# A tuned H3 and MLP kernel: the statistics between two units from accumulator sums and powers, gating in stages, weights split ahead of the chain, products paused

## The chip, the core and the metric

The kernel runs on one core of a Trainium2 chip. The metric is device time in microseconds (us) of one execution. The core has five engines with a queue each: TensorE (PE; PEld is its loading of weights), VectorE (DVE), ScalarE (ACT), GpSimd (POOL) and SyncE (SP), which here issues the DMAs. Each works through its queue in order, and waits at an instruction until what it reads is there and the buffer that it writes is free. So an instruction that waits holds up all that stands behind it on its engine.

## The reference

Two layers, each of a mixer (A) and an MLP (B), on 2048 tokens of 1024 features in float32, with the same weights in both layers.

```
def _A_ref(q, k, v, shift_k, ssm_k, ssm_D):
    ...
    kv = k_shift * v
    ...
    y = y + kv * ssm_D[None, None, :]
    return q * y
def _B_ref(x, w1, b1, w2, b2):
    h = jnp.einsum("bsd,df->bsf", x, w1) + b1
    zero = jnp.zeros_like(h)
    r = jnp.where(h > zero, h, zero)
    h = r * r
    out = jnp.einsum("bsf,fd->bsd", h, w2) + b2
    return out
...
x = A_q
x = x + _A_ref(_layernorm(x, axis=-1), A_k, A_v, A_shift_k, A_ssm_k, A_ssm_D)
x = x + _B_ref(_layernorm(x, axis=-1), B_w1, B_b1, B_w2, B_b2)
x = x + _A_ref(_layernorm(x, axis=-1), A_k, A_v, A_shift_k, A_ssm_k, A_ssm_D)
x = x + _B_ref(_layernorm(x, axis=-1), B_w1, B_b1, B_w2, B_b2)
```

What is left out makes `k_shift`, a causal convolution of k with 4 taps, and `y`, a causal convolution of kv with ssm_k over all 2048 tokens, by FFT. `y` depends on k, v, ssm_k and ssm_D alone, not on x, so both layers use the same one.

## The kernel before

**Units.** The tokens are cut into four blocks of 512, a block into four tiles of 128. A unit is the MLP of one layer on one block. The table `ORDER` (L36) gives their order: (layer 0, block 0), (layer 1, block 0), (layer 0, block 1) and so on; the last two blocks of layer 1 end together. Units 0 and 1 have the same block: unit 1 needs what unit 0 gives, through a mixer and two layernorms. Only between these two does the **chain** (L1727) run.

**Steps.** A unit is a list of steps. A step of kind m1 (first product) or m2 (second) has 12 matmuls of 128x512 in units 0 and 1: each float32 factor is split into a high and a low part, and three of the four products are added (`mm3`, L355 to L358). At the end of unit 0 its last 28 steps are half steps: for two tiles (tiles 0 and 1, the first half) and then for the other two, with 6 matmuls each. Then follow 24 half steps of unit 1's m1, with 12 matmuls of half the width: 12 on the first two tiles, which do not need the other two, and 12 on those. The first 8 steps of unit 0 in the main loop are half steps too.

**Weights.** `w_advance` loads a weight by DMA, casts it to its high part on ACT (L1112), and subtracts to get the low part (the split, L1120) on DVE or POOL, by a table `WLO` and the phase: DVE in full steps and in the first half's m2, POOL in the second half's m2 (phase "b"), and POOL for three of four in the ahead steps of m1 (phase "x"). Some weights were stored split and come back whole (`whl<-wd_m`). The split runs three steps ahead of the matmuls (five in phase "x"), as far as six buffers `whl` allow.

**The chain.** At the end of a half, the result is added to the accumulator `acc` in two parts (`evict1`). Then mean and variance of the two tiles give a scale, y gates the scaled tile, the product is added, a second layernorm follows, and the normalized tiles are transposed and split into `xh` and `xl` for unit 1. These are stages, which `lag.at(d, stage, ...)` puts d steps later into the program; `lag.tick()` writes out what is due at a step. `CHAIN` (L67) holds the delays of the eleven stages for the first and for the second half.

**Beside it** run two streams, a piece per step. The forward stream (L374 to L515) transforms k, v and ssm_k for later blocks: on DVE three multiply-adds L386 and a product L388 into `fx`, which PE transposes (L441) into a bank `pt`, and for ssm_k the sums L504 and L505. The product stream (L540) multiplies the spectra on POOL (L546), reduces on DVE (L550), and ends in matmuls L616. `PACE_SLACK` sets how many steps it shall be done ahead of time; from it comes `pace`, the work per step. In half steps the loop's end takes a tenth of it:

```
rate = pace.get(u, 100) * (PREP_PACE if busy else 1.0)
if len(tts) < NT:
    rate *= 0.1
owed += rate
todo = min(owed, BURST * rate)
while todo > 0:
    x = next(pds, 0)
```

A product that is not ready to go gives None there, and the forward stream moves one piece on.

Of the kernel before, what the change touches and what calls it, by code (L numbers as in the profile page):

```python
# [20 lines left out]
P = 128  # L21
# [28 lines left out]
PACE_SLACK = {1: 74, 3: 10}  # L50
PACE_TO = {1: 2}
PLAIN = 1
PAD_C, PAD_P, PAD_M = 104, 56, 32
# [13 lines left out]
CHAIN = ((2, 3, 3, 7, 8, 8, 9, 13, 13, 14, 14), (2, 3, 3, 7, 8, 8, 9, 12, 12, 13, 13))  # L67
NORM = "VAVA"
# [181 lines left out]
def tile_h3_mlp(ctx: ExitStack, tc: tile.TileContext, q, kT, vT, shk, ssmT, ssmD, w1, b1, w2, b2,  # L250
# [1476 lines left out]
    def chain(accs, b, xh, xl, ready):  # L1727
        def bn(st, h):
            for n, tt in enumerate(st["tts"]):
                V.bn_stats(st["st"][:, n, h], accs[tt][:, h * 512:(h + 1) * 512])  # L1730

        def agg(st):
            mv = st["mv"] = pre.tile([P, 2, 2], F32, name="mv3", bufs=2)
            for n in range(2):
                V.bn_aggr(mv[:, n], st["st"][:, n])
            st["ve"], st["sd"] = rstd_a(mv)

        def newst(st):
            st["st"] = pre.tile([P, 2, 2, 6], F32, name="st3", bufs=2)

        def scales(st):
            r = st["r"] = rstd_b(st["ve"], st["sd"])
            st["nm"] = pre.tile([P, 2], F32, name="nm", bufs=3)
            V.scalar_tensor_tensor(st["nm"], st["mv"][:, :, 0], -1.0, r, op0=OP.mult, op1=OP.mult)

        def scaled(st, n):
            out = []
            for h in range(2):
                z = ps1()
                A.activation(z, accs[st["tts"][n]][:, h * 512:(h + 1) * 512], AF.Identity,  # L1750
                             bias=st["nm"][:, n:n + 1], scale=st["r"][:, n:n + 1])
                out.append((h, z, accs[st["tts"][n]][:, h * 512:(h + 1) * 512], st["y"][n][:, h * 512:(h + 1) * 512]))
            return out

        def gate(ops):
            for h, z, x, y in ops:
                V.tensor_mul(z, z, y)
            for h, z, x, y in ops:
                V.tensor_add(x, x, z)

        def spread_of(st, n, ops):
            for h, z, x, y in ops:
                V.bn_stats(st["st"][:, n, h], x)

        def evict1(st, os, dh):
            d = slice(dh * 512, (dh + 1) * 512)
            for n, tt in enumerate(st["tts"]):
                V.tensor_add(accs[tt][:, d], os[tt], accs[tt][:, d])
                V.bn_stats(st["st"][:, n, dh], accs[tt][:, d])

        def stage(st, k):
            tts = st["tts"]
            if k == 0:
                agg(st)
            elif k == 1:
                scales(st)
                newst(st)
            elif k == 2:
                ops = scaled(st, 0)
                gate(ops)  # L1780
                more = scaled(st, 1)
                spread_of(st, 0, ops)
                gate(more)
                spread_of(st, 1, more)
            elif k == 3:
                agg(st)
            elif k == 4:
                scales(st)
            elif k in (5, 6):
                n = k - 5  # L1790
                x, m, r = accs[tts[n]], st["mv"][:, n, 0:1], st["r"][:, n:n + 1]
                st["o", n] = []
                st["z", n] = [row() for _ in range(2)]
                for kh in range(2):
                    xn = st["z", n][kh]["t"]
                    xs = x[:, kh * 512:(kh + 1) * 512]
                    if NORM[2 * n + kh] == "A":
                        A.activation(xn, xs, AF.Identity, bias=st["nm"][:, n:n + 1], scale=r)
                    else:
                        V.tensor_scalar(xn, xs, m, r, op0=OP.subtract, op1=OP.mult)  # L1800
                    st["o", n].append(xn)
# [10 lines left out]
            else:  # L1812
# [552 lines left out]
```

## Time and profile before

| what | us |
|---|---|
| median of 3 runs (lowest, highest) | 2678.97 (2678.12, 2685.03) |
| the profiled execution | 2684.3 |
| its span, first to last instruction | 2682.5 |

The profile is of that one execution. Times within it are counted from the start of the span. Two stretches bear on the change: the main part of unit 0 with the end of the block before it, and the half steps with the chain.

| stretch, us | PE busy | DVE busy | ACT busy | POOL busy | PE clock granted |
|---|---|---|---|---|---|
| 130 to 450 | 307.82 | 265.12 | 140.98 | 176.75 | 0.98 |
| 450 to 560 | 101.25 | 84.45 | 50.68 | 42.49 | 0.97 |

A row of the timeline gives the start, the time taken, engine, line, operation, the tiles written and read, and in brackets how long the engine stood idle before it and what ended that. Matmuls overlap, so the time from one start to the next is what one costs. In the list of waits an entry gives total, times and longest.

### The profile page before, as it was taken

Reading aid. Unit: us, or ns where it says so; the run is one execution under the profiler, and the core shown is the slowest. Engines: PE = TensorE matmul, PEld = TensorE weight load, DVE = VectorE, ACT = ScalarE, POOL = GpSimd, SP = SyncE. Lnnn points to the kernel's source line nnn. Section 1 sums busy time; section 2 is a strip of 40 time slices with the busy share of each in tenths; the row PEclk is TensorE's granted clock in tenths of the full one; section 3 lists DMA queues with packets and bytes.
Section 4 is the critical chain, followed back from the end, with each engine's and each line's share of the span. In section 5 each row is a group of like instructions: output and inputs, shape, how many; then the busy total and the mean of one; then the engine's idle time right before and its main releaser. Section 6 shows DMA issues by size and latency. Waiting matters only on the chain.

```text
span 2682.5 us, 36122 instructions
## 1 busy us (share of the span) xinstructions
PE 2623.8 (98%) x12388; PEld 2199.4 (82%) x12388; DVE 1985.1 (74%) x2881; ACT 1124.1 (42%) x1915; POOL 1034.1 (39%) x675
## 2 busy tenths in 40 slices
PE   7999899899999999999999999999999999999999
PEld 6888787787888888888888888888788778888887
DVE  7979788788887878779767775456778668777553
ACT  3444244343435323343233422345444585454342
POOL 2436665155551744417454275100100217536111
PEclk9999999999999999999999999999999999999999
DMA  7789988689989998888987888689889797878653
GB/s 247 255 306 310 296 291 283 240 282 357 348 296 315 313 331 307 275 292 308 337 307 261 297 292 314 201 273 312 299 298 307 263 340 255 263 249 316 232 193 121
DMA packets 380265, 763.16 MB, mean 284 GB/s; under 512 B 44064, under 2 KB 159408, under 8 KB 377008
## 3 DMA queue, kind: packets, MB, share of 16 engines
q1 hardware_dynamic: 380080, 760.85, 83.0%
q8 instruction: 98, 1.61, 0.2%
q14 instruction: 87, 0.71, 0.1%
HBM read 583.49 MB, written 177.21 MB: 284 GB/s over the span
## 4 chain that ended last, share of the span: by engine, by line
PE 79%; DMA 8%; DVE 5%; POOL 2%; issue 2%; ACT 2%; SPq 1%; DVEq 0%; POOLq 0%; ACTq 0%
PE p L357 23%; PE p L356 23%; PE p L358 23%; DMA whl<-wd_m 2%; PE pt L358 2%; PE pt L357 2%; PE pt L356 2%; PE p L1194 2%; DMA wr<-w 2%; DMA cg<-gd 1%; DVE whl L1120 1%; POOL cp L546 1%; DMA wd_m<-whl 0%; PE p L817 0%; DVE sm L550 0%
## 5 line engine op out<-in xcount | busy, mean ns | idle before, releaser
L546 POOL TENSOR_TENSOR cp<-cx,cg 128x384 f32<-128x384 f32 (+5 forms) x288 | 542.0, 1895 | 574.7 <-DVE sm L550 362.2
L356 PE MATMUL p<-xh,whl 128*128 128x512 f32 (+1 forms) x1504 | 578.4, 385 | 5.6 <-DMA whl<-wd_m 5.6
L358 PE MATMUL p<-xh,whl 128*128 128x512 f32 (+1 forms) x1504 | 574.1, 382 | 3.3 <-DVE whl L1120 2.8
L357 PE MATMUL p<-xl,whl 128*128 128x512 f32 (+1 forms) x1504 | 574.1, 382 | 0.1
L1112 ACT CAST whl<-wr 128x512 fp32r<-128x512 f32 x546 | 332.5, 619 | 468.4 <-PE p L358 278.6
L1120 DVE TENSOR_TENSOR whl<-wr,whl 128x512 fp32r<-128x512 f32 x486 | 421.0, 877 | 135.0 <-ACT whl L1112 130.2
L356 PE MATMUL p<-whl,rh 128*128 128x512 f32 x1204 | 475.4, 395 | 6.0 <-DMA whl<-wd_m 5.2
L357 PE MATMUL p<-whl,rh 128*128 128x512 f32 x1204 | 471.2, 391 | 2.8 <-POOL whl L1120 1.7
L358 PE MATMUL p<-whl,rl 128*128 128x512 f32 x1204 | 470.6, 391 | 0.0
L356 PEld LDWEIGHTS p<-xh,whl 128*128 128x128 f32 x1504 | 284.7, 189 | 60.8 <-issue 4.9
L358 PEld LDWEIGHTS p<-xh,whl 128*128 128x128 f32 x1504 | 284.2, 189 | 58.2 <-DVE whl L1120 3.0
L357 PEld LDWEIGHTS p<-xl,whl 128*128 128x128 f32 x1504 | 284.5, 189 | 52.4 <-DVE xl L1507 0.3
L1597 DVE TENSOR_TENSOR rl<-wr,rh 128x512 fp32r<-128x512 f32 x140 | 138.6, 990 | 182.5 <-ACT rh L1594 182.4
L1120 POOL TENSOR_TENSOR whl<-wr,whl 128x512 fp32r<-128x512 f32 x60 | 86.7, 1448 | 484.4 <-ACT whl L1112 438.1
L356 PEld LDWEIGHTS p<-whl,rh 128*128 128x128 f32 x1204 | 227.3, 189 | 54.1 <-issue 3.3
L357 PEld LDWEIGHTS p<-whl,rh 128*128 128x128 f32 x1204 | 227.1, 189 | 50.2 <-DVE whl L1120 2.7
L358 PEld LDWEIGHTS p<-whl,rl 128*128 128x128 f32 x1204 | 227.0, 189 | 47.5
L550 DVE TENSOR_REDUCE sm<-cp 128x128 f32<-128x384 f32 (+5 forms) x288 | 249.4, 874 | 12.3 <-POOL cp L546 12.3
L1589 ACT ACTIVATE wr<-p,b1t 128x512 f32<-128x512 f32 x138 | 95.2, 690 | 371.9 <-PE p L358 371.0
L1717 DVE TENSOR_TENSOR acc<-p,acc 128x512 f32<-128x512 f32 x152 | 99.7, 686 | 81.3 <-PE p L358 81.3
L696 POOL TENSOR_TENSOR sm<-sm 128x512 f32<-128x512 f32 x48 | 69.1, 1440 | 132.4 <-DVE sm L550 118.8
L358 PE MATMUL p<-whl,tq 128*128 128x512 f32 x276 | 107.4, 389 | 0.0
(384 smaller groups left out, 4282.3 us busy)
## 6 DMA issues: line engine op xcount, KB each, us to landing
whl<-wd_m SPq DMA_DIRECT2D x318, 512.0 KB, 5.6
wr<-w SPq DMA_DIRECT2D x442, 256.0 KB, 5.6
wd_m<-whl SPq DMA_DIRECT2D x70, 512.0 KB, 6.1
wr<-td SPq DMA_DIRECT2D x112, 256.0 KB, 5.1
cx<-xd SPq DMA_DIRECT2D x48, 512.0 KB, 5.7
cg<-gd SPq DMA_DIRECT2D x48, 512.0 KB, 7.0
tq<-hd SPq DMA_DIRECT2D x24, 1024.0 KB, 6.9
gd<-fg SPq DMA_DIRECT2D x72, 256.0 KB, 6.7
```

Of the source, the lines that this page charges most:

```text
L356: PE.matmul(o, lh, rh, start=start, stop=False)
L357: PE.matmul(o, lh, rl, start=False, stop=False)
L358: PE.matmul(o, ll, rh, start=False, stop=stop)
L546: G.tensor_mul(pr.rearrange("p c i -> p i c"), xt[:, 0:j + 1], gt[:, j::-1])
L550: V.tensor_reduce(sm[:, ty, jj], st["pr"], axis=AX.X, op=OP.add)
L696: E.tensor_add(s[:, 1:3], s[:, 1:3], s[:, 0:1].to_broadcast([P, 2, s.shape[2]]))
L1112: A.copy(t[:, 0], raws[n]["t"])
L1120: ENG[e[n % len(e)]].tensor_sub(t[:, 1], raws[n]["t"], t[:, 0].bitcast(F32))
L1194: PE.matmul(o, lh, r, start=start, stop=stop)
L1589: A.activation(r, st["o"], AF.Relu, bias=b1t[:, st["f"]:st["f"] + 1])
L1597: V.tensor_sub(st["lo"], st["r"]["t"], st["hi"].bitcast(F32))
L1717: V.tensor_add(accs[tt][:, d], o, accs[tt][:, d])
```

## The change

- `evict1` adds the first tile of a half with an instruction that also sums what it writes (`summed`), for both parts; from the two sums come the mean (one small DVE instruction) and, by a squaring pass on ACT with a sum (`spread_a`), the variance. The second tile keeps bn_stats (`spread_v`). After the gating it is the same again.
- The scale is a power on POOL (three small instructions, `scale_of`) for each tile, in place of a square root on ACT and six small instructions on DVE for both.
- The gating is two stages, one tile each (`CHAIN` 3 and 5), with the scales of the first layernorm kept in `old`. The first tile is normalized at 6 and the second at 9; in the second half the transposes are at 11 and 12, where both were at 12. Both halves of the first tile are normalized on ACT (`NORM`).
- In every half step `w_advance` comes ahead of `lag.tick()`; before, this was so in phase "x" alone.
- In half steps the products' rate is nought; `PACE_SLACK` for units 0 to 2 is 80 where it was 74. A pad of memory grows.

```diff
-PACE_SLACK = {1: 74, 3: 10}
+PACE_SLACK = {1: 80, 3: 10}
...
-PAD_C, PAD_P, PAD_M = 104, 56, 32
+PAD_C, PAD_P, PAD_M = 104, 72, 32
...
-CHAIN = ((2, 3, 3, 7, 8, 8, 9, 13, 13, 14, 14), (2, 3, 3, 7, 8, 8, 9, 12, 12, 13, 13))
-NORM = "VAVA"
+CHAIN = ((2, 3, 5, 7, 8, 6, 9, 13, 13, 14, 14), (2, 3, 5, 7, 8, 6, 9, 11, 12, 12, 13))
+NORM = "AAVA"
...
+        def summed(st, n, d, z):
+            x = accs[st["tts"][n]][:, d * 512:(d + 1) * 512]
+            V.scalar_tensor_tensor(x, z, 1.0, x, op0=OP.mult, op1=OP.add, accum_out=st["c"][:, 4 + d:5 + d])
+
+        def spread_a(st):
+            c = st["c"]
+            V.tensor_scalar(c[:, 0:1], c[:, 4:5], c[:, 5:6], -1.0 / (root * D), op0=OP.add, op1=OP.mult)
+            junk = ml.tile([P, D], BF16, name="yt", bufs=2)
+            A.activation(junk, accs[st["tts"][0]], AF.Square, scale=1.0 / root, bias=c[:, 0:1], accum_out=c[:, 1:2])
+            scale_of(st, 0, c[:, 1:2], c[:, 0:1], root)
+
+        def spread_v(st):
+            mv = pre.tile([P, 1, 2], F32, name="mv3", bufs=2)[:, 0]
+            V.bn_aggr(mv, st["st"][:, 0])
+            scale_of(st, 1, mv[:, 1:2], mv[:, 0:1], -1.0)
+
+        def scale_of(st, n, var, m, k):
+            o = st["rn"][:, n]
+            G.tensor_add(var, var, epst)
+            G.tensor_tensor(o[:, 0:1], var, eph[:, 1:2], op=OP.pow)
+            G.tensor_scalar(o[:, 1:2], m, o[:, 0:1], k, op0=OP.mult, op1=OP.mult)
...
         def evict1(st, os, dh):
             d = slice(dh * 512, (dh + 1) * 512)
-            for n, tt in enumerate(st["tts"]):
-                V.tensor_add(accs[tt][:, d], os[tt], accs[tt][:, d])
-                V.bn_stats(st["st"][:, n, dh], accs[tt][:, d])
+            t0, t1 = st["tts"]
+            summed(st, 0, dh, os[t0])
+            if dh == (t0 > 0) ^ 1:
+                spread_a(st)
+            V.tensor_add(accs[t1][:, d], os[t1], accs[t1][:, d])
+            V.bn_stats(st["st"][:, 0, dh], accs[t1][:, d])
...
             elif k == 1:
-                scales(st)
+                st["g"] = scaled(st, 0)
+                st["old"] = dict(st)
                 newst(st)
+                gate(st, 0, st["g"])
+                spread_a(st)
             elif k == 2:
-                ops = scaled(st, 0)
-                gate(ops)
-                more = scaled(st, 1)
-                spread_of(st, 0, ops)
-                gate(more)
-                spread_of(st, 1, more)
+                gate(st, 1, scaled(st["old"], 1))
             elif k == 3:
-                agg(st)
-            elif k == 4:
-                scales(st)
+                for h in range(2):
+                    V.bn_stats(st["st"][:, 0, h], accs[tts[1]][:, h * 512:(h + 1) * 512])
+                spread_v(st)
...
-        if phase[0] == "x":
+        if len(tts) < NT:
             w_advance(s, top)
             lag.tick()
...
         if len(tts) < NT:
-            rate *= 0.1
+            rate = 0.0
```

Three places show how instructions move. The first is DVE's queue in unit 0, before a transpose of the forward stream. In the kernel before, these rows run from the last of four evictions (L1717) to the product L388 that PE's L441 waits for, in the trace from 293 to 304 us.

```order
L1717 TENSOR_TENSOR acc<-p_2582,acc 128x512
L1120 TENSOR_TENSOR whl<-wr,whl 128x512
L550 TENSOR_REDUCE sm<-cp 128x128
L504 TENSOR_TENSOR fg<-pt,fg 128x2x2x64
L505 TENSOR_TENSOR fg<-pt,fg 128x2x2x64
L386 SCALAR_TENSOR_TENSOR fx<-fx,shkt 128x512 x3
L504 TENSOR_TENSOR fg<-fk 128x2x2x64
L505 TENSOR_TENSOR fg<-fk 128x2x2x64
L1120 TENSOR_TENSOR whl<-wr,whl 128x512
L388 TENSOR_TENSOR fx<-fx 128x512
```

In the changed kernel the transpose with the most DVE work in front of it is the second of unit 0; its rows, again from the last eviction on:

```order
L1717 TENSOR_TENSOR acc<-p_1636,acc 128x512
L1120 TENSOR_TENSOR whl<-wr,whl 128x512
L386 SCALAR_TENSOR_TENSOR fx<-fx,shkt 128x512 x3
L504 TENSOR_TENSOR fg<-pt,fg 128x2x2x64
L505 TENSOR_TENSOR fg<-pt,fg 128x2x2x64
L388 TENSOR_TENSOR fx<-fx 128x512
```

The forward stream has shifted against the steps: a reduction, a pair of sums and a split no longer stand between eviction and product here.

The second place is POOL's queue from the last products of unit 0 on. In the kernel before, the splits of the second half's weights (L1120) stand there among products.

```order
L696 TENSOR_TENSOR sm<-sm 128x512
L1120 TENSOR_TENSOR whl<-wr,whl 128x512 x5
L546 TENSOR_TENSOR cp<-cx,cg 128x4x128
L700 TENSOR_TENSOR sm<-sm 128x256
L701 TENSOR_TENSOR sm<-sm 128x4x64
L1120 TENSOR_TENSOR whl<-wr,whl 128x512 x2
L546 TENSOR_TENSOR cp<-cx,cg 128x3x128
L1120 TENSOR_TENSOR whl<-wr,whl 128x512
```

In the changed kernel the first half's chain stands there (L1748 to L1750 are the scale of one tile, `nr` the first tile's column, `mv` the second's).

```order
L1748 TENSOR_TENSOR mv_4651<-mv_4651,eph 128x1
L1749 TENSOR_TENSOR mv_4550<-mv_4651,eph 128x1
L1750 TENSOR_SCALAR mv_4550<-mv_4651,mv_4550 128x1
L1120 TENSOR_TENSOR whl<-wr,whl 128x512
L1748 TENSOR_TENSOR nr<-nr,eph 128x1
L1749 TENSOR_TENSOR mv_4669<-nr,eph 128x1
L1750 TENSOR_SCALAR mv_4669<-nr,mv_4669 128x1
L1120 TENSOR_TENSOR whl<-wr,whl 128x512
L1748 TENSOR_TENSOR mv_4729<-mv_4729,eph 128x1
L1749 TENSOR_TENSOR mv_4669<-mv_4729,eph 128x1
L1750 TENSOR_SCALAR mv_4669<-mv_4729,mv_4669 128x1
L1120 TENSOR_TENSOR whl<-wr,whl 128x512 x3
```

The products are gone from these rows, and each of the first splits stands behind statistics. The last row's first split is for the eleventh half step after the chain's begin.

The third place is DVE's queue in the second half. In the kernel before, from the gating of the first tile (L1757) to the split that PE waits for at 521 us:

```order
L1757 TENSOR_TENSOR p_4978<-p_4978,px 128x512
L1757 TENSOR_TENSOR p_4980<-p_4980,px 128x512
L1759 TENSOR_TENSOR acc<-acc,p_4978 128x512
L1759 TENSOR_TENSOR acc<-acc,p_4980 128x512
L1763 BN_STATS st_4977<-acc 128x6 x2
L1757 TENSOR_TENSOR p_4986<-p_4986,px 128x512
L1757 TENSOR_TENSOR p_4988<-p_4988,px 128x512
L1759 TENSOR_TENSOR acc<-acc,p_4986 128x512
L1759 TENSOR_TENSOR acc<-acc,p_4988 128x512
L1763 BN_STATS st_4977<-acc 128x6 x2
L1120 TENSOR_TENSOR whl<-wr,whl 128x512
```

The same place in the changed kernel:

```order
L1769 TENSOR_TENSOR p_4902<-p_4902,px 128x512
L1769 TENSOR_TENSOR p_4904<-p_4904,px 128x512
L1732 SCALAR_TENSOR_TENSOR acc,nr<-p_4902,acc 128x512
L1732 SCALAR_TENSOR_TENSOR acc,nr<-p_4904,acc 128x512
L1736 TENSOR_SCALAR nr<-nr 128x1
L1120 TENSOR_TENSOR whl<-wr,whl 128x512
L1769 TENSOR_TENSOR p_4951<-p_4951,px 128x512
L1769 TENSOR_TENSOR p_4953<-p_4953,px 128x512
L1772 TENSOR_TENSOR acc<-acc,p_4951 128x512
L1772 TENSOR_TENSOR acc<-acc,p_4953 128x512
L1812 BN_STATS st_4906<-acc 128x6 x2
L1743 BN_AGGR mv_4997<-st_4906 128x2
```

The split stands between the gating of the two tiles, with five instructions in front of it instead of twelve.

More of the change, by code (lines that the diff above doesn't have):

```diff
@@ L1727, in chain @@
     def chain(accs, b, xh, xl, ready):
[L1728 to L1744 removed]
+        root = math.sqrt(D)
+        def summed(st, n, d, z):
[16 more added lines that the diff above has]
+            G.tensor_scalar(o[:, 1:2], m, o[:, 0:1], k, op0=OP.mult, op1=OP.mult)
+        def newst(st):
+            st["st"] = pre.tile([P, 1, 2, 6], F32, name="st3", bufs=2)
+            st["c"] = pre.tile([P, 6], F32, name="nr", bufs=4)
+            st["rn"] = pre.tile([P, 2, 2], F32, name="mv2", bufs=4)
         def scaled(st, n):
@@ L1811, in stage @@
                 drop(*st["z", n])
-            else:
+            elif k > 8:
                 n = k - 9
```

47 lines of the change are left out of this document (24 added, 23 removed).

## The prediction

> **What bounds the kernel now.** First the page, for the shares; then the list of what the engines waited for; then the timeline of TensorE (PE) at each of those places. The page leaves little to gain.
>
> ```profile
> span 2682.5 us, 36122 instructions
> PE 2623.8 (98%) x12388; PEld 2199.4 (82%) x12388; DVE 1985.1 (74%) x2881; ACT 1124.1 (42%) x1915; POOL 1034.1 (39%) x675
> ```
>
> PE is busy 98% of the span, and the change takes no matmul away. It can only remove time in which PE stands still or runs slowly, 58.7 us in all, and of that only what lies where it moves instructions: unit 0 (until about 450 us) and the chain between units 0 and 1 (473 to 532 us). Of the three rows below, from the list of PE's waits (us in total, times, longest), the second and third are unit 0's; the first is for weights that come by DMA, all but one of them after the chain.
>
> ```profile
> PE p L356 <- DMA whl<-wd_m: 10.8, 9, 2.9
> PE pt L441 <- DVE fx L388: 9.8, 4, 7.3
> ...
> PE pt L616 <- DVE fg L505: 2.4, 1, 2.4
> ```
>
> Four transposes of the forward stream (L441) waited 9.8 us for a product on VectorE (DVE, L388), one of them 7.3; a product's matmul (L616) waited 2.4. The timeline shows what follows such a wait.
>
> ```profile
> 263.62 0.72 PE L441 MATMUL pt<-ident,fx 128*128 128x128 f32 x4 [1.86 <-DVE fx L388]
> ...
> 304.15 1.10 PE L441 MATMUL pt<-ident,fx 128*128 128x128 f32 x4 [7.26 <-DVE fx L388]
> 304.90 0.77 PE L356 MATMUL p<-whl,rh 128*128 128x512 f32 x1
> ...
> 309.74 0.45 PE L358 MATMUL p<-whl,rl 128*128 128x512 f32 x1
> ...
> 449.09 1.39 PE L616 MATMUL pt<-sm,yh 128*128 128x128 f32 x8 [2.35 <-DVE fg L505]
> 450.13 0.77 PE L356 MATMUL p<-xh,whl 128*128 128x512 f32 x1
> ...
> 453.25 0.40 PE L357 MATMUL p<-xl,whl 128*128 128x512 f32 x1
> ...
> 453.71 0.39 PE L356 MATMUL p<-xh,whl 128*128 128x512 f32 x1
> 453.94 0.39 PE L357 MATMUL p<-xl,whl 128*128 128x512 f32 x1
> ```
>
> At full speed a 128x512 matmul starts 0.23 us after the one before (453.71, 453.94). After the wait of 7.26 us eleven intervals take 4.84 us (304.90 to 309.74) where 2.50 are due: 2.3 us lost to a halved clock. After 2.35 us of waiting seven intervals take 3.12 instead of 1.59: 1.5 lost. After 1.86 us nothing is lost. So unit 0 loses 9.8 + 2.4 + 2.3 + 1.5 = **16.0 us**. The longest of these waits is a pile-up on DVE:
>
> ```profile
> 291.54 2.48 DVE L1717 TENSOR_TENSOR acc<-p,acc 128x512 f32<-128x512 f32 x4
> ...
> 295.79 3.67 DVE L386 SCALAR_TENSOR_TENSOR fx<-fx,shkt 128x512 f32<-128x512 f32 x3
> 299.38 1.21 DVE L504 TENSOR_TENSOR fg<-fk 128x256 f32<-128x256 f32 x1
> 300.52 1.49 DVE L505 TENSOR_TENSOR fg<-fk 128x256 f32<-128x256 f32 x1
> 301.93 1.48 DVE L1120 TENSOR_TENSOR whl<-wr,whl 128x512 fp32r<-128x512 f32 x1
> ```
>
> Four evictions stand in front, and the next four rows, with L388 right behind them, take up to three times what like ones take elsewhere, with GpSimd (POOL) multiplying beside them. Now the chain on PE.
>
> ```profile
> 476.81 0.50 PE L357 MATMUL p<-whl,rh 128*128 128x512 f32 x1 [0.72 <-DVE whl L1120]
> ...
> 494.31 0.50 PE L357 MATMUL p<-whl,rh 128*128 128x512 f32 x1 [0.84 <-POOL whl L1120]
> ...
> 497.28 0.51 PE L356 MATMUL p<-whl,rh 128*128 128x512 f32 x1 [0.18 <-ACT whl L1112]
> ...
> 498.63 0.50 PE L357 MATMUL p<-whl,rh 128*128 128x512 f32 x1 [0.84 <-POOL whl L1120]
> ...
> 500.66 0.50 PE L356 MATMUL p<-whl,rh 128*128 128x512 f32 x1 [0.60 <-DMA whl<-wd_m]
> ...
> 521.28 0.43 PE L358 MATMUL p<-xh,whl 128*128 128x256 f32 x1 [2.79 <-DVE whl L1120]
> ...
> 524.92 0.28 PE L357 MATMUL pt<-xl,whl 128*128 128x256 f32 x1
> ...
> 530.39 1.25 PE L1809 MATMUL p<-ident,wr 128*128 128x128 f32 x8 [0.97 <-DVE xl L1818]
> ```
>
> Five waits in the first half make 3.18 us, and its second transposes wait another 0.97, as those of the second half do in the last row: 4.15. Each stop costs some 0.28 more while PE starts up again (497.28 to 498.63 is 1.35, of which 0.84 is the next wait and 0.23 a matmul), so six stops make 5.8. The second half waits 2.79 + 0.97, two starts 0.5, and from 521.28 to 524.92 seventeen half-width intervals take 3.64 instead of 17 x 0.12 = 2.04: 1.6. That is 5.9, and the chain loses **11.7 us**.
>
> **The change, part by part.** Durations for the new line of statistics come from these rows.
>
> ```profile
> 487.97 1.49 ACT L1750 ACTIVATE p<-acc,nm,rs 128x512 f32<-128x512 f32 x2 [1.87 <-DVE nm L1744]
> ...
> 492.30 0.60 ACT L1112 CAST whl<-wr 128x512 fp32r<-128x512 f32 x1
> ...
> 2142.10 1.15 ACT L723 ACTIVATE jk<-px,co 128x1024 bf16<-128x1024 f32 x1
> 2143.15 0.19 ACT L723 ACTIVATION_READ_ACCUMULATOR jk<-px,co 128x1 f32 x1
> ...
> 2143.42 0.19 POOL L724 TENSOR_TENSOR co<-co,eph 128x1 f32<-128x1 f32 x1 [10.88 <-ACT jk L723]
> 2143.69 0.56 POOL L725 TENSOR_TENSOR co<-co,eph 128x1 f32<-128x1 f32 x1
> 2144.22 0.23 POOL L1880 TENSOR_SCALAR co<-co 128x1 f32<-128x1 f32 x1
> ...
> 486.18 1.28 POOL L1120 TENSOR_TENSOR whl<-wr,whl 128x512 fp32r<-128x512 f32 x1 [21.98 <-DVE rt L747]
> ...
> 486.21 1.27 DVE L741 TENSOR_SCALAR rt<-rt 128x2 f32<-128x2 f32 x1
> ...
> 488.78 1.40 DVE L1757 TENSOR_TENSOR p<-p,px 128x512 f32<-128x512 f32 x2 [0.91 <-ACT p L1750]
> 490.09 1.27 DVE L1759 TENSOR_TENSOR acc<-acc,p 128x512 f32<-128x512 f32 x2
> 491.29 1.28 DVE L1763 BATCH_NORM_STATS2 st<-acc 128x6 f32<-128x512 f32 x2
> ...
> 496.06 0.33 DVE L1735 BATCH_NORM_AGGREGATE mv<-st 128x2 f32<-128x12 f32 x2
> ```
>
> *The sum taken while adding* (L1732). The trace shows no DVE instruction with an accumulator. Its cost lies between a plain add (0.64, half of 1.27) and an add with the bn_stats that it replaces (1.28). I take 0.84, the add and the accumulator read that ScalarE (ACT) shows.
>
> *First half.* From the first eviction on, the line is: sum 0.84 and a small op 0.2 (as half of L1735's two) on DVE; square and read 1.34 on ACT; three POOL ops, 2143.42 to 2144.45, 1.03; one scaling 0.75; two products 1.35, two sums 1.68, a small op 0.2 on DVE; square and read 1.34, a weight cast 0.60 and a scaling 0.75 on ACT; then for the other tile two products 1.35, two adds 1.27, two bn_stats 1.28 and bn_aggr 0.2 on DVE. That is 14.2, and with some 0.05 for each of nine handovers 14.6. Behind it come three POOL ops (1.03) and only then, on POOL, the split of the weight for the eleventh half step: ready at 16.9. PE wants it ten steps of six matmuls after the eviction, 10 x 6 x 0.23 = 13.8, plus a start-up and an earlier wait of about 0.8, since the ninth step's split stands on POOL behind the first tile's second statistics. So **a new wait of about 2.0 us** (0 to 3.5) takes the place of those at 494 and 498. The wait at 476.81 goes: that split now stands ahead of the eviction, with three DVE instructions behind it instead of four. The transposes keep theirs, and the wait for DMA is covered by the new one. Sum 0.5 + 2.0 + 0.97 and three starts = 4.3, so 1.5 of 5.8 are gained.
>
> *Second half.* The split that PE waited for at 521.28 stood on DVE behind the gating of both tiles; now it stands behind that of one (two products, two sums, a small op), and is done about 8 us after the half's first step, where PE wants it after seven steps of 12 x 0.12 = 1.44, at 10. That wait and its slow clock go, 2.79 + 0.28 + 1.6. Late next are the transposes: the first tile's come one step earlier, the second's follow after a step of matmuls, so most of their 0.97 is hidden; but the first tile's casts on ACT now queue behind the second tile's normalization, and I leave 0.7 and a start. Sum 1.0; 4.9 of 5.9 gained. **The chain gains 6.4** (2 to 9).
>
> *Products paused, and pace.* In a half step the rate was a tenth and is now nought; over units 0 to 2 the pace in full steps rises from a total over 250.4 steps to one over 244.4, 2.5% more work per step on POOL and DVE. The pause also begins at once, in the eight half steps that open unit 0, and keeps the forward stream still there, so every L441 and L616 in unit 0 stands elsewhere. What that does I read from the order: the DVE work that stands between the split which PE needs anyway and the row it waits for, each at its undisturbed duration (0.6 for full rows, 0.34 for half ones). In the kernel before it is 10.4 us at the wait of 7.26, 9.1 at that of 2.35, and 6.7 or less at the seven other transposes, which waited 2.5 together. In the changed one the largest are 8.5, 8.5, 7.9, 7.9 and 7.4. Between 0.36 (2.5 over seven) at 6.7 and 2.35 at 9.1 a straight line gives 1.9, 1.9, 1.4, 1.4 and 1.0, and 0.36 for each of four others: 9.0, with no halved clock. **Unit 0 gains 7.0.** Ends: nothing left to wait for (16 gained), or as at 304 in two places (4 lost).
>
> The padding, the scratch tile and the normalization moved to ACT cost nothing where ACT is idle, as 1.87 us ahead of 487.97 shows.
>
> **How the sum stands.** 7.0 + 6.4 = 13.4. The profiled execution took 2684.3 us (span 2682.5) and would take 2670.9; the median of the runs shown is 2679.0, and I make the forecast against it: **2665.6**.
>
> **The rivals.**
> - *The waits of unit 0 only move.* The forward stream stays tied to DVE, and 2.5% more products make it later; then 16.0 stay and only the chain's 6.4 are gained: 2672.6. For it: four waits at four different places. Against: no place has 10.4 us in front of it any more.
> - *POOL holds the weights back.* With the sum at 1.28 the line in the first half is 1.3 longer, the wait 3.3, and the clock halves (1.5, as after 2.35): the chain gains 3.6, the time is 2668.4. The Trainium skill, page "TensorE: Matmul & The Clock Gate", Part 1, sets the fall to half speed at about 3.4 us of idleness; by it this rival would keep full speed and end at 2666.9, but the waits of 2.35 and 2.79 here were followed by half speed, so the rows decide.
> - *DVE and POOL block each other (slower).* At 486.18 and 486.21 a small DVE op lasted 1.27 us, exactly as long as a POOL split beside it, and the rows at 295.79 to 301.93 stretched the same way. The Trainium skill, page "SBUF — State Buffer", section "Who interferes with whom", calls this an exclusive lock on a shared port pair, taken by DVE instructions with two SBUF inputs; the trace agrees. Products squeezed into full steps meet the forward stream more often. Each of the five large places that goes as at 304 costs 7.3 + 2.3 = 9.6. Three of five make 28.8, and some 4.2 at the other places (two of 1.4, four of 0.36), against 16.0 before and less the chain's 6.4: 10.6 slower, 2689.6. It decides from three on.
> - *Nothing comes of it.* The pause is paid back by other waits further on (units 1 and 2, by more waits for DMA like those of the first row of the list, nine with 10.8 us): 2679.
>
> **How the numbers follow.** Forecast 0.55, waits only move 0.20, POOL 0.08, blocking 0.07, nothing 0.10. What a measurement of this kernel can tell from no change is about 0.3%, 8 us, so faster is below 2671. The forecast and the POOL rival lie there nearly always, of the first rival a quarter: 0.66. Slower 0.07, the rest 0.27 the same. The range reaches from unit 0 without waits and no new wait on POOL (2655) to the case of nothing (2679).
>
> **What would show it.** Right: no wait over 2.4 us at L441 before 450 us, no DVE wait near the chain's second half, a wait of 1 to 3 us on a POOL split in the first half. Wrong: a wait of 5 us or more in unit 0, half clock after the POOL wait, or new waits for whl by DMA in units 1 and 2.

## The result, and the profile after

The changed kernel takes 2707.34 us (median of four runs, 2700.72 to 2711.33), the kernel before in the same comparison 2680.11 (2678.12 to 2685.03): a ratio of 1.0103, 95% interval 1.009 to 1.0116. It is **1% slower**, where 0.5% faster was forecast. The profiled execution took 2700.7, the fastest of the four.

The page of the changed kernel: the span and the busy time of each engine.

```profile
span 2698.9 us, 36084 instructions
...
PE 2627.0 (97%) x12388; PEld 2199.9 (82%) x12388; DVE 1987.4 (74%) x2851; ACT 1128.7 (42%) x1921; POOL 1045.3 (39%) x699
```

The same matmuls, 16.4 us more span. Where PE stood still shows the view of windows: the stretch, its length, then the busy time of each engine. First the kernel before, then the changed one.

```profile
460.00:560.00 100.00, 91.25 (x545) 79.51 (x544) 74.49 (x126) 46.55 (x78) 35.45 (x24) 0.98 0.70 241
560.00:1290.00 730.00, 726.82 (x3446) 610.36 (x3445) 596.07 (x820) 280.48 (x502) 347.49 (x199) 1.00 0.90 315
```

```profile
460.00:560.00 100.00, 91.23 (x557) 80.35 (x557) 63.69 (x95) 51.96 (x86) 46.23 (x48) 1.00 0.71 241
560.00:1290.00 730.00, 716.10 (x3384) 599.51 (x3383) 601.96 (x809) 276.20 (x496) 350.20 (x203) 0.99 0.89 311
```

Behind the chain, in units 1 and 2, PE was idle 3.2 us of 730 before and is idle 13.9 now. Idle time alone leaves out the slow clock, so the table adds up lost time: for each matmul the interval to the next one, less an undisturbed interval of its form (the one that three in ten stay below). Each column is one profiled execution; the second one of the changed kernel and the last two columns are runs told below.

| lost on PE, us | before | changed | changed, second profile | new chain alone | pause alone |
|---|---|---|---|---|---|
| 0 to 130 | 43.7 | 41.4 | 40.1 | 42.9 | 41.1 |
| 130 to 460, unit 0 | 31.9 | 32.7 | 34.9 | 29.7 | 30.8 |
| 460 to 560, the chain | 13.8 | 11.5 | 14.4 | 8.3 | 14.0 |
| 560 to 1290, units 1 and 2 | 9.0 | 23.9 | 27.7 | 6.3 | 25.4 |
| 1290 to the end | 22.8 | 28.4 | 29.3 | 22.2 | 28.2 |
| all | 121.2 | 137.9 | 146.5 | 109.5 | 139.5 |

Of the 16.7 us between the first two profiles, 14.9 are lost in units 1 and 2 and 5.6 later, less what the start and the chain gain. In units 1 and 2 the waits for DVE grew most: they make 10.7 us where they made 0.5. Waits for DMA there are 3.1 against 2.7, and the rest is mostly slow clock. From 1290 us on no wait for DVE has grown; there PE waits for DMA 10.0 us against 7.6, and the clock is slower behind these waits. The prediction's gains were to come from unit 0, which has none, and from the chain, which has a part. The list of PE's waits in the changed kernel:

```profile
PE p L356 <- DMA whl<-wd_m: 13.1, 7, 4.5
...
PE pt L441 <- DVE fx L388: 8.3, 3, 3.8
PE p L357 <- DVE whl L1120: 4.9, 4, 2.2
PE pt L357 <- DVE fx L402: 4.7, 1, 4.7
PE p L1823 <- DVE xl L1832: 3.6, 2, 2.8
PE p L357 <- POOL whl L1120: 2.9, 2, 2.2
PE pt L616 <- DVE fg L505: 2.7, 1, 2.7
PE p L356 <- DVE acc L1717: 2.6, 1, 2.6
```

L441 still waits 8.3 us (9.8 before) and L616 2.7 (2.4). L402 and L1717 are new among the long ones. In the timeline of PE, unit 0 and the chain:

```profile
237.68 0.71 PE L441 MATMUL pt<-ident,fx 128*128 128x128 f32 x4 [3.81 <-DVE fx L388]
...
314.38 0.74 PE L441 MATMUL pt<-ident,fx 128*128 128x128 f32 x4 [2.50 <-DVE fx L388]
...
349.64 0.72 PE L441 MATMUL pt<-ident,fx 128*128 128x128 f32 x4 [2.00 <-DVE fx L388]
...
496.09 0.50 PE L357 MATMUL p<-whl,rh 128*128 128x512 f32 x1 [2.22 <-POOL whl L1120]
...
502.55 1.26 PE L1823 MATMUL p<-ident,wr 128*128 128x128 f32 x8 [2.76 <-DVE xl L1832]
...
524.06 1.15 PE L1823 MATMUL p<-ident,wr 128*128 128x128 f32 x7 [0.80 <-DVE xl L1832]
...
634.59 0.50 PE L358 MATMUL p<-xh,whl 128*128 128x512 f32 x1 [1.17 <-DVE whl L1120]
...
650.62 0.58 PE L357 MATMUL pt<-fx,fh 128*128 128x256 f32 x1 [4.67 <-DVE fx L402]
...
1178.69 0.50 PE L356 MATMUL p<-whl,rh 128*128 128x512 f32 x1 [2.61 <-DVE acc L1717]
...
1252.87 0.50 PE L357 MATMUL p<-whl,rh 128*128 128x512 f32 x1 [2.21 <-DVE whl L1120]
```

The one wait of 7.26 us in unit 0 has become three of 2 to 4. The chain is near to what was drawn, but for the transposes at 502. The last four rows are the 10.7 us in units 1 and 2, and the kernel before has no such wait at these places. POOL and DVE ahead of the wait at 650 show how it arises (start, time, engine).

```profile
638.20 1.74 POOL L696 TENSOR_TENSOR sm<-sm 128x512 f32<-128x512 f32 x1
639.90 2.03 POOL L546 TENSOR_TENSOR cp<-cx,cg 128x640 f32<-128x640 f32 x1
641.88 1.19 POOL L700 TENSOR_TENSOR sm<-sm 128x256 f32<-128x256 f32 x1
643.15 1.25 POOL L701 TENSOR_TENSOR sm<-sm 128x256 f32<-128x256 f32 x1
644.36 5.32 POOL L546 TENSOR_TENSOR cp<-cx,cg 128x768 f32<-128x768 f32 x3
```

```profile
646.25 0.95 DVE L550 TENSOR_REDUCE sm<-cp 128x128 f32<-128x768 f32 x1 [2.44 <-POOL cp L546]
647.12 2.84 DVE L582 TENSOR_TENSOR yl<-sm,yh 128x256 fp32r<-128x256 f32 x2
649.88 0.68 DVE L402 TENSOR_TENSOR fx<-pt,fx 128x512 fp32r<-128x512 f32 x1
```

Three sums of the product stream stand ahead of a product on POOL; DVE waits 2.44 us for that product at the head of its queue; then two small subtractions take 2.84 us beside the next product (0.74 for a pair at 634 us in the new chain alone); and behind them stands L402, for which PE waits. No piece is new. They meet here and did not before.

The largest wait behind 1290 us, 4.50 for a weight by DMA at 1932 us, comes when both side streams have ended (POOL's last product starts at 1689 us). SyncE issues the loads in order, and there it stands 10.5 us at a load of x (L753) until POOL has read the buffer (L1694); it issues that load at 1926.11 and the next weight's at 1926.54. In the kernel before it stands 8.0 us at the same load, and PE waits 1.07. How the change reaches POOL's work there was not followed up.

### The profile page after: what moved, and what is told of

Same layout as the page of the kernel before. It is cut to its first block, busy times and chain, and to the rows that moved or that the text cites. A ratio compares the mean times of both kernels' runs of the same rounds, so it can differ in the third digit from the quotient of the medians.

```text
span 2698.9 us, 36084 instructions
## 1 busy us (share of the span) xinstructions
PE 2627.0 (97%) x12388; PEld 2199.9 (82%) x12388; DVE 1987.4 (74%) x2851; ACT 1128.7 (42%) x1921; POOL 1045.3 (39%) x699
## 4 chain that ended last, share of the span: by engine, by line
PE 74%; DMA 9%; DVE 8%; issue 3%; POOL 3%; ACT 2%; SPq 2%; DVEq 0%; ACTq 0%; POOLq 0%
PE p L356 21%; PE p L358 21%; PE p L357 21%; PE p L1194 2%; PE pt L357 2%; PE pt L358 2%; PE pt L356 2%; DMA wr<-w 2%; DMA whl<-wd_m 2%; DMA cg<-gd 2%; DVE whl L1120 1%; DVE sm L550 1%; POOL cp L546 1%; DVE fx L386 1%; POOL acc L1854 1%
## 5 line engine op out<-in xcount | busy, mean ns | idle before, releaser
L1120 DVE TENSOR_TENSOR whl<-wr,whl 128x512 fp32r<-128x512 f32 x486 | 417.4, 870 | 135.6 <-ACT whl L1112 130.2
L1597 DVE TENSOR_TENSOR rl<-wr,rh 128x512 fp32r<-128x512 f32 x140 | 151.5, 1083 | 175.0 <-ACT rh L1594 174.6
L1120 POOL TENSOR_TENSOR whl<-wr,whl 128x512 fp32r<-128x512 f32 x60 | 87.1, 1454 | 435.4 <-ACT whl L1112 231.0
L1717 DVE TENSOR_TENSOR acc<-p,acc 128x512 f32<-128x512 f32 x152 | 99.9, 687 | 70.4 <-PE p L358 70.4
```

The source lines that it names most:

```text
L1120: ENG[e[n % len(e)]].tensor_sub(t[:, 1], raws[n]["t"], t[:, 0].bitcast(F32))
L1597: V.tensor_sub(st["lo"], st["r"]["t"], st["hi"].bitcast(F32))
L1717: V.tensor_add(accs[tt][:, d], o, accs[tt][:, d])
```

## The experiments

**The parts apart.** "New chain alone" is the changed kernel with the old pause and pace, "pause alone" the kernel before with the new ones.

```
# new chain alone: from the changed kernel
-PACE_SLACK = {1: 80, 3: 10}
+PACE_SLACK = {1: 74, 3: 10}
-            rate = 0.0
+            rate *= 0.1
# pause alone: the same lines the other way, from the kernel before
# weights split as before: from the changed kernel
-        if len(tts) < NT:
+        if phase[0] == "x":
```

> The changed kernel with the pause undone: in half steps the product stream keeps its tenth of the rate, and the pace its old divisor (slack 74); the new chain, the weights split first and the padding stay. Theory A (the pause and the pace put the two side streams against other steps, and the loss arises after the chain, in units 1 and 2): the time is that of the kernel before or some microseconds less, 2670 to 2682, and the waits at 650 us (4.67) and 1178 us (2.61) are gone. Theory B (the new chain, with its longer waits of 2.22 and 2.76 us in the first half, costs it): the loss stays, 2698 to 2710.

> The kernel before with nothing but the pause and its pace (rate nought in half steps, slack 80); the old chain. Theory A (side streams): slower than before by most of the 27 us, 2698 to 2710, with waits in units 1 and 2 that the kernel before hasn't. Theory B (new chain): as before, 2675 to 2684.

> The changed kernel with one part undone: weights are split ahead of the chain's due work in the half steps of unit 1 alone, as before, and no longer in those of unit 0. Theory A (side streams) and theory B (chain's statistics) both expect the changed kernel's time, 2700 to 2711, with up to 3 us more in the first half of the chain. Theory C (splitting first delays the forward stream and the evictions and that is what costs): 2680 to 2690.

> The changed kernel once more, to see how far its own executions differ. Its profiled execution took 2700.7 us and its others 2706 to 2711, at granted clocks of 0.994 and 0.991 to 0.992. Theory A with chance in it (each wait of some 1.7 to 2.9 us is followed by half a clock in some executions and not in others): the waits stand at the same places within 1 us, and the times lost behind them (1.7 each) differ from those of the first profile. Theory D (waits for DMA come and go): the waits themselves differ by several microseconds.

| run | median, us | ratio to before (2679.16) |
|---|---|---|
| new chain alone | 2673.59 | 0.9984 (0.9976 to 0.9993) |
| pause alone | 2703.55 | 1.0094 (1.0082 to 1.0106) |
| splits as before | 2700.85 | 1.0082 (1.0069 to 1.0095) |
| changed again | 2704.07 | 1.0092 (1.0078 to 1.0105) |

This settles which part does it. The chain gains 5.6 us by the medians; the pause with its pace costs 24.4; theory B falls. Theory C falls too: with the splits as before the time is within 3.3 us of the changed kernel's, where 2680 to 2690 was expected. The two parts do not add up: 24.4 less 5.6 is 18.8, and the changed kernel, at 2704.07, is 24.9 slower than the one before. With the pause in place the new chain gains nothing that these runs can tell (2704.07 against 2703.55). The windows of new chain alone, then of pause alone:

```profile
460.00:560.00 100.00, 94.15 (x574) 82.77 (x574) 68.33 (x101) 53.06 (x88) 46.17 (x49) 1.00 0.74 255
560.00:1290.00 730.00, 728.51 (x3458) 611.37 (x3457) 606.30 (x822) 280.52 (x501) 352.95 (x201) 1.00 0.91 317
```

```profile
460.00:560.00 100.00, 89.65 (x546) 77.94 (x545) 72.90 (x123) 45.03 (x75) 38.29 (x25) 1.00 0.70 238
560.00:1290.00 730.00, 715.97 (x3377) 598.54 (x3376) 600.76 (x808) 275.51 (x494) 350.79 (x202) 0.99 0.89 310
```

With the old chain and the pause, PE idles 14.0 us behind the chain, as in the changed kernel; with the new chain and no pause, 1.5.

The second profile of the changed kernel has most of its long waits at the same places of the program (the wait for L1717 is 2.61 in both), while the clock behind them differs. A few waits differ by more than a microsecond: the one at 634 us is 2.48 for 1.17, and at 474 stands 2.31 for ACT where the first has 0.86 for DVE. For the wait for L1717, first profile, then second:

```profile
1178.69 0.50 PE L356 MATMUL p<-whl,rh 128*128 128x512 f32 x1 [2.61 <-DVE acc L1717]
...
1180.63 0.39 PE L358 MATMUL p<-whl,rl 128*128 128x512 f32 x1
1180.86 0.39 PE L356 MATMUL p<-whl,rh 128*128 128x512 f32 x1
```

```profile
1183.05 0.50 PE L356 MATMUL p<-whl,rh 128*128 128x512 f32 x1 [2.61 <-DVE acc L1717]
...
1184.88 0.63 PE L356 MATMUL p<-whl,rh 128*128 128x512 f32 x1
1185.31 0.63 PE L357 MATMUL p<-whl,rh 128*128 128x512 f32 x1
```

Intervals of 0.23 in the one, 0.43 in the other, after the same wait. This differs from run to run, and is most of why the first profile (clock 0.994, 2700.7) was kinder than the median (0.991 to 0.992 in the other runs): from 130 us on the second profile lost 6.2 us more between waits and 3.6 more at them.

**Pause, pace, or place?** Four variants of the changed kernel, the step limit (24, since AHEAD_0 is 4) lying behind the eight half steps that open unit 0.

```
# slack 78:         rate = 0.0, PACE_SLACK = {1: 78, 3: 10}
# pace alone:       rate *= 0.1                                     (slack 80)
# pause at chain:   rate *= 0.1 if s < 16 + 2 * AHEAD_0 else 0.0    (slack 79.2)
# pause at start:   rate *= 0.0 if s < 16 + 2 * AHEAD_0 else 0.1    (slack 74.8)
```

> The changed kernel, pause and all, with a slack of 78 in place of 80: the pace of the products in full steps is 0.8% lower, so both side streams stand a little later against the steps, more so the further on. If the loss comes of the pause itself (a backlog that has to be caught up), the time stays, 2698 to 2709, with the waits at about 634, 650, 1178 and 1252 us at their places. If it comes of where single instructions of the streams happen to stand (chance alignment), those waits vanish or move, and the time lies anywhere from 2670 to 2710.

> The changed kernel with a tenth of the rate kept in half steps and the slack of 80: the new pace (2.5% more products in each full step) with no pause. If the squeeze into full steps is what costs (GpSimd and VectorE run later than TensorE needs them), 2690 to 2705. If the pause costs, the time is that of the new chain alone, 2671 to 2679.

> The changed kernel with the pause only in the 52 half steps before and in the chain; in the eight that open unit 0 the tenth of the rate stays (slack 79.2, which keeps the sum of the work). If the loss comes of the pause at the chain, 2698 to 2709 with the waits behind the chain (634, 650 us); if it comes of the stream's place from the start on, 2671 to 2682, and the waits of unit 0 stand where they do without the pause (262 and 302 us).

> The changed kernel with the pause only in the eight half steps that open unit 0; at the chain the tenth of the rate stays (slack 74.8). If the loss comes of the pause at the chain, 2671 to 2680. If it comes of the streams' new place from the start on, 2695 to 2709.

| run | median, us | 95% interval of the ratio to before (2679.14) |
|---|---|---|
| slack 78 | 2704.70 | 1.0084 to 1.0115 |
| pace alone | 2695.92 | 1.0055 to 1.0083 |
| pause at the chain | 2689.32 | 1.0032 to 1.0057 |
| pause at the start | 2706.33 | 1.0084 to 1.0112 |

Every one is slower than both kernels with the old pace, and each in its own way. With slack 78 the time stays, as if the pause itself cost it, but the waits do not: those at 650 and 1252 us are gone, the one at 1178 is down to 1.39, and new ones of 2.54 (at 706, for DVE's L424) and 3.28 (at 1328, for DMA) have come. The pause at the chain came out between the two times expected. So neither the pace nor either pause was "the" cause, and the next question was whether the old pace is only a lucky place.

**Other paces, with no pause.** New chain alone, with its slack of 74 changed to 73, 75 and 77; and a chain with two numbers set anew.

```
# slack 73, 75, 77: PACE_SLACK = {1: 73, 3: 10}, and so on
# chain set anew (slack 74):
-CHAIN = ((2, 3, 5, 7, 8, 6, 9, 13, 13, 14, 14), (2, 3, 5, 7, 8, 6, 9, 11, 12, 12, 13))
+CHAIN = ((2, 3, 5, 8, 8, 6, 9, 12, 13, 13, 14), (2, 3, 5, 7, 8, 6, 9, 11, 12, 12, 13))
```

> The new chain with the tenth of the rate kept in half steps and a slack of 73 (with 74: 2673.6): a pace 0.4% lower. If the squeeze is what costs (the more products in each full step, the later GpSimd and VectorE are; 2695.9 at 80), there is a little to gain or nothing to lose: 2671 to 2675. If it is chance alignment of the side streams with the steps, in which 74 happens to be a good number, it is slower: 2678 to 2700.

> The same with a slack of 75: a pace 0.4% higher. Squeeze: a sixth of the way from 2673.6 at 74 to 2695.9 at 80, 2674 to 2680. Chance alignment: no order between 73, 75, 77 and 80, anywhere from 2672 to 2700, with waits for VectorE that stand at other places in each.

> The same with a slack of 77: a pace 1.2% higher. Squeeze: half of the way, 2682 to 2688. Chance alignment: anywhere from 2672 to 2700, not in order with the others.

> The new chain with the old pause and pace (2673.6), and in its first half two numbers changed: the second tile's statistics one step later, so that GpSimd splits one more weight ahead of them, and the first tile's transposes and casts one step earlier, ahead of a step of matmuls. If the wait of 2.23 us at 495 is GpSimd's order alone, it goes with its start-up of 0.3, and the 1.28 at the transposes nearly so: 2669 to 2671. If the line of statistics itself is what PE waits for, the wait turns up at the transposes, and the time stays at 2672 to 2675.

| new chain, no pause, slack | 73 | 74 | 75 | 77 | 80 |
|---|---|---|---|---|---|
| median, us | 2691.05 | 2673.59 | 2681.95 | 2690.92 | 2695.92 |
| lost on PE, 560 to 1290 | 14.4 | 6.3 | 4.4 | 18.0 | 15.0 |

A pace 0.4% lower, with less squeeze, costs 17 us, and one 0.4% higher 8. The squeeze cannot explain 73. Nor does the loss keep to one stretch: 75 has none of it in units 1 and 2, but loses 14.5 us instead of 8.3 from 460 to 560. Nor do the long waits of units 1 and 2 keep their places: at 73 the longest, 1.95 for DVE, stands at 692 us, at 77 one of 3.09 for ACT at 842, at 80 one of 3.04 for DVE at 639, and at 75 there is none over 0.7. At 74 the streams pass each other well, and every other pace that was tried loses that. The chance-alignment theory, with its "anywhere from 2672 to 2700", fits all five. But from 74 up the times rise in order, which that theory did not expect; so a price of the squeeze on top is not ruled out, and 73 alone speaks for chance in the times.

The chain set anew takes 2673.07 (0.9964 to 0.9985 of before). The wait of 2.23 for POOL's split is gone from the timeline of its first half. The earlier one, 0.82 in the new chain alone, is down to 0.41; one of 0.59 for a weight by DMA and the transposes' are left:

```profile
488.47 0.50 PE L357 MATMUL p<-whl,rh 128*128 128x512 f32 x1 [0.41 <-POOL whl L1120]
...
494.11 0.50 PE L356 MATMUL p<-whl,rh 128*128 128x512 f32 x1 [0.59 <-DMA whl<-wd_m]
...
496.86 1.26 PE L1823 MATMUL p<-ident,wr 128*128 128x128 f32 x8 [1.10 <-DVE xl L1832]
```

The chain lost 6.3 us instead of 8.3, so the wait of 2.23 was GpSimd's order alone. The time does not show it: the medians differ by 0.5 us where 2669 to 2671 was expected, and in this profile 2.1 us more were lost behind 1290. Both kernels beat the one before, by 0.2%.

**Has the pause at the start a price of its own?** All kernels with it had come out at 2701 to 2707, the others but 74 at 2682 to 2696. Three more paces with it, and two runs that leave the pause in but give the forward stream one extra turn in each of the eight full steps behind it:

```
# start 72, start 77: as pause at start, slack 72.8 and 77.8;  pause, slack 83: the changed kernel with 83
# turns back (pause at the start alone, slack 74; and the changed kernel, slack 80):
+        if 2 * AHEAD_0 + 8 <= s < 2 * AHEAD_0 + 16:
+            fwd_tick()
         owed += rate
```

> New chain, pause only in the eight half steps that open unit 0, slack 72.8 (with 74.8: 2706.3). A price of its own for that pause: 2698 to 2710. The same chance as without it: anywhere from 2674 to 2706, with waits at other places.

> The same with slack 77.8. A price of its own: 2698 to 2710. The same chance: anywhere from 2674 to 2706.

> The changed kernel, pause and all, with slack 83 (with 80: 2704 to 2707; with 78: 2704.7). A price of its own for the pause at the start: 2698 to 2712. The same chance: anywhere from 2676 to 2712.

> New chain, pause only in the eight half steps that open unit 0, and the forward stream given one extra turn in each of the eight full steps behind them (slack 74). If the eight lost turns are the price of that pause, its time is that of kernels without it: 2674 to 2693, and 135 or more products are done before 462 us. If the price lies elsewhere in the pause: 2698 to 2711 as before (2706.3 without the turns).

> The changed kernel, pause and all and slack 80, with the eight extra turns. If the lost turns are the price: 2682 to 2696, as with the pause at the chain alone (2689.3). If not: 2700 to 2710 as the changed kernel.

| run | median, us | 95% interval of the ratio to before |
|---|---|---|
| start 72 | 2698.36 | 1.006 to 1.0088 |
| start 77 | 2710.90 | 1.011 to 1.0143 |
| pause, slack 83 | 2704.86 | 1.0083 to 1.011 |
| turns back, pause at the start alone | 2689.64 | 1.0024 to 1.0049 |
| turns back, changed kernel | 2705.48 | 1.0083 to 1.0114 |

The first three fit a price of the pause within a microsecond, but the same chance as without it allowed two of them too; only start 77 lies outside its range. Eight kernels with the pause at the start and nothing given back lie at 2698 to 2711, above all five that have no such pause and another pace than 74 (2682 to 2696). The nearest two of the groups, 2698.36 and 2695.92, have intervals that overlap. With the pause at the start alone the times, too, rise with the pace (2698, 2706 and 2711 at slacks of 72.8, 74.8 and 77.8). What the pause does to the product stream is plain from the products on POOL before 462 us: new chain alone, the changed kernel, turns back (pause at the start alone).

```profile
L546 POOL TENSOR_TENSOR cp<-cx,cg x91: 995/1312/1765, 191.1 to 458.1; 128x384 f32<-128x384 f32 x46, 128x512 f32<-128x512 f32 x45
```

```profile
L546 POOL TENSOR_TENSOR cp<-cx,cg x84: 1012/1318/2024, 202.9 to 446.8; 128x384 f32<-128x384 f32 x42, 128x512 f32<-128x512 f32 x42
```

```profile
L546 POOL TENSOR_TENSOR cp<-cx,cg x90: 1003/1312/2278, 193.7 to 460.4; 128x384 f32<-128x384 f32 x45, 128x512 f32<-128x512 f32 x45
```

In those eight half steps no product is ready, and each call of the product stream with a rate above nought moves the forward stream one piece on. With a rate of nought it isn't called: the first product comes at 203 instead of 191 us, and 84 instead of 91 are done before the chain, so the rest lies in units 1 and 2. (The expectation's "135 or more" counts semaphore rows too; products alone are 90 to 92 without that pause and 84 to 87 with it.) Giving the turns back restores the 90 in both runs, but the time in one only: 2689.6 against 2706.3, and 2705.5 against 2704 to 2707. The first of these comparisons is not of the turns alone, since the slack is 74 in the one run and 74.8 in the other, and a step of 1 moved the time by 8 to 17 us above. The second, at one slack, finds no price of the lost turns: a kernel with 90 products takes 2705 too. So it is not shown that the backlog costs.

## Why the prediction was wrong

- **What bounds it**: right. All differences are waits of PE and the clock behind them. But the 58.7 us "in which PE stands still or runs slowly" are idle time alone; a slow matmul counts as busy, and the table above, which holds both, has 121.2.
- **The chain** was to gain 6.4 us; alone it gained 5.6 by the medians, 5.5 in lost time (13.8 to 8.3). The sum with accumulator was put at 0.84, and takes 0.73 to the start of what follows it:

```profile
479.76 0.68 DVE L1732 SCALAR_TENSOR_TENSOR acc<-p,acc 128x512 f32<-128x512 f32 x1
480.37 0.08 DVE L1732 DVE_READ_ACCUMULATOR acc<-p,acc 128x1 f32 x1
480.49 0.21 DVE L1736 TENSOR_SCALAR nr<-nr 128x1 f32<-128x1 f32 x1
```

  The new wait on POOL's split was put at 2.0 and is 2.22; the split was to be ready 16.9 us after the first eviction and was so after 16.3 (479.76 to 496.1). The clock kept full speed behind it in the changed kernel's profiles, but 1.75 us were lost behind the same wait (2.23) with slack 78, so whether POOL halves the clock, as that rival has it, differs from run to run. The DVE wait of the second half went, with its slow clock, and the transposes there wait 0.80 for the 0.7 that were left. The earlier wait for a split on POOL, put at 0.5 in the sum, is 0.72 (0.82 in the new chain alone). Three terms were off in the changed kernel, and less or not at all with the old pace. The wait for DVE at 476 was to go; it went in the new chain alone, and 0.86 stands at 474.88 in the changed kernel. A wait of 0.53 for POOL's split at 550 us has grown to 1.42 (0.51 in the new chain alone). And the second transposes wait 2.76, not 0.97, since the casts that release them stood on ACT behind weight casts that waited for DMA, the last of them 1.34 us (in the new chain alone these casts ran some 1.5 us earlier in the chain, and the transposes wait 1.28):

```profile
500.67 0.62 ACT L1112 CAST whl<-wr 128x512 fp32r<-128x512 f32 x1 [1.34 <-DMA wr<-w]
501.19 1.07 ACT L1831 CAST xh<-p 128x512 fp32r<-128x512 f32 x2
```

- **Unit 0** was to gain 7.0; it lost 0.8 more (31.9 to 32.7). Here a first step failed. The DVE work ahead of a transpose did shrink as read from the order, and the longest wait with it (7.26 to 3.81), but the straight line through two waits gave 1.9, 1.9, 1.4 and 1.4 where 3.81, 2.50 and 2.00 came at L441 and 2.66 at L616, the longest with a halved clock behind it. The kernel before had already shown that DVE's own work does not set the wait: its third point, 7.26 with 10.4 us in front, lies 3.8 above the line. At the wait of 3.81, at 237 us, DVE stood idle 2.39 us for a product on POOL, and POOL had stood idle 3.08 before its products for an operand by DMA:

```profile
230.68 2.28 POOL L546 TENSOR_TENSOR cp<-cx,cg 128x384 f32<-128x384 f32 x2 [3.08 <-DMA cg<-gd]
...
231.73 0.56 DVE L550 TENSOR_REDUCE sm<-cp 128x128 f32<-128x384 f32 x1 [2.39 <-POOL cp L546]
```

  The first rival, that unit 0's waits only move, is what happened there. Its 2672.6 is within a microsecond of the new chain alone, but that is luck as to unit 0: that run has neither the pause nor the pace.
- **Products paused, and pace** was costed in unit 0 only, and put at nothing behind it. That is the error that turned the sign: the forward stream runs on to some 1460 us and the products to some 1690, and the pause moved all of both. The rival "nothing comes of it" named the place, units 1 and 2, but only as waits for DMA and sized to cancel the gain, 13.4, at a chance of 0.10; it was 14.9 there and 5.6 later. In units 1 and 2 it was hardly DMA (3.1 us for 2.7) but DVE (10.7 for 0.5): at 650 and 1178 us as shown, and ahead of the wait at 1252 three multiply-adds L386 take 7.11 us beside POOL's work, where three at their median take 2.3. The 5.6 behind are waits for DMA and ACT and the clock behind them. The slower rival, blocking in unit 0, had the right mechanism for units 1 and 2 at the wrong place. Of the rows with which it argues, the one at 486.21 (L741, 1.27 us) is not of an instruction with two inputs, as it reads one tensor; those at 295.79 to 301.93 read two. What remains open is why the streams meet badly: by their place alone, by the squeeze of the pace, or by both.
- **The padding, the normalization on ACT and the splits first** were put at nothing. Of these only the splits were undone alone (3.2 us between the medians, which the intervals, 1.0069 to 1.0095 and 1.0078 to 1.0105, do not tell apart); the others are in the new chain's sum.
- What was to show it: the second half and the POOL wait came out right, "no wait over 2.4 us at L441" wrong at once. Of the three signs of being wrong none came clearly: no wait of 5 us in unit 0, full speed after the POOL wait, and hardly more waits for weights by DMA in units 1 and 2.

## What to carry to other kernels

When work that runs beside the bounding engine is free to slide, a change of its rate is a change of every later place where it meets something; cost it over all of its length, or pin it to the steps, and don't count a gain at two places as the sum. Measure such a change apart from the rest, and at two or three neighbouring rates: here five paces within 3% of each other spread over 22 us, four times what the new chain gained. A schedule that was good for the old stream can be lost with it, so a part that gains by itself (the new chain) should first be tried with the old rates.

## What the hardware showed

**A wait of two microseconds can cost nearly twice that, in some runs and not in others.** Over the 19 profiles of these runs, from 130 us on, PE's waits were sorted by length, and those counted behind which more than 1.3 us were lost to slow matmuls (intervals without a wait) within 6 us:

| wait, us | 0.75 to 1.6 | 1.6 to 1.9 | 1.9 to 2.5 | 2.5 to 4 | over 4 |
|---|---|---|---|---|---|
| waits | 145 | 42 | 90 | 60 | 20 |
| with a slow clock behind | 0 | 11 | 51 | 52 | 20 |

The prediction took it that 1.86 us costs nothing and 2.35 halves the clock. In these profiles none of 0.75 to 1.6 us has a slow clock behind it, every one over 4 has, and between it can go either way. The Trainium skill, page "TensorE: Matmul & The Clock Gate", Part 1, has the clock watched in free-running windows of about 3.4 us and halved after an idle one. That the same wait of 2.61 us has either outcome agrees with windows that run free; that 1.6 to 2.5 us often suffices differs from it, and the counts decide.

**A one-element instruction can hold the queue.** Ahead of the wait at 1178 us in the changed kernel, on DVE and POOL:

```profile
1175.99 0.15 DVE L741 TENSOR_SCALAR rt<-rt 128x1 f32<-128x1 f32 x1
1176.18 1.74 DVE L742 TENSOR_TENSOR rs<-rs,rt 128x1 f32<-128x1 f32 x1
1177.84 0.20 DVE L758 TENSOR_SCALAR nm<-mv 128x1 f32<-128x1 f32 x2
1177.96 1.27 DVE L1717 TENSOR_TENSOR acc<-p,acc 128x512 f32<-128x512 f32 x2
```

```profile
1175.80 2.11 POOL L546 TENSOR_TENSOR cp<-cx,cg 128x896 f32<-128x896 f32 x1
```

L742 multiplies one number per partition. It ends with POOL's product, at 1177.9. In the kernel before and in the new chain alone, none of its 29 and 25 executions took more than 0.17 us. L741 in front of it, which reads one tensor of the same size, took 0.15 us beside the same product. PE waited 2.61 for the eviction behind L742, and the hold is some 1.6 us of that. The prediction priced such blocking at 9.6 a place and looked for it in unit 0; behind the chain it came at single places, with waits of 2 to 5 us.
